# A delta-rule recurrence rewritten in 32-token chunks on small TensorE tiles, ahead of a mixture of experts

## The chip, the cores and the metric

The kernel runs on one NeuronCore of a Trainium2 chip. The engines are PE (TensorE, with its weight loads shown as PEld), DVE (VectorE), ACT (ScalarE), POOL (GpSimd) and SP, which here only issues DMAs and reads a few registers. The metric is device time in microseconds (us) of one execution; the kernel before took a median of 550.71 us in three runs (546.65 to 550.84).

## The reference

Attention by the delta rule, then a top-1 mixture of experts on its output. Everything is fp32. Batch 4, 8 heads, 768 tokens, head width 48; the model width is 8 x 48 = 384, with 8 experts of width 1024 and 3072 tokens in all.

```python
k_n = k / (norm(k) + 1e-6)
for t in range(S):                       # state: (B, H, 48, 48)
    y[:, :, t] = q_t @ state
    v_old      = k_n_t @ state
    state     += beta_t * outer(k_n_t, v_t - v_old)
x = y as 3072 rows of 384                # batch, token; heads side by side
logits = x @ w_gate + modality_bias[modality_id]
e = argmax(logits); g = softmax(logits)[e]
out = g * (relu(x @ w1[e]) @ w2[e])
```

Token by token the recurrence would be 768 serial steps. In chunks it becomes, per head: the Gram matrix of the chunk's keys, the inverse R of a unit triangular matrix made from it and beta, then Z = R (V - K S) with the state S before the chunk, Y = Q S + P Z with P the masked product of queries and keys, and S + K'Z for the next chunk.

## The kernel before

**Recurrence** (class `Attention`). A chunk is 64 tokens, so there are 12 chunks, each in two *group steps* of two batches and all heads: 24 steps `i=2c+g`. `gram` (L100 to L145) multiplies block-diagonal copies of the keys with keys and queries (L124, one matmul for two heads on the full array) and sorts the products into Gram blocks and P. `inverse_` (L154 to L238) works on sets of two chunks: six sets. Set 0 is inverted in blocks of 16 columns that `join` (L240) joins on PE with 32x32 and 16x32 tiles; the other five are inverted in blocks of 32 columns, one column after the other (L213 multiplies, L214 subtracts), rows 0 to 11 of the result on DVE and the rest on POOL. Sets 0 and 1 are laid out by transposes and copies, sets 2 to 5 go through DRAM (`GD`, `RD`, `RE`). `level_` (L314) joins blocks of 32 to blocks of 64 on PE (L326, L335). `chain_` (L348) is the serial part of a step: `ks` (K S, L363), `RHS` (V less it, DVE L365), `z` (L378), its copy `ZT` (ACT), the state's sum in PSUM (`Sps`, L386), its copy `Sbd` (ACT, L391), and beside it `y` (L372, L394), its copy `xo` and its store to DRAM (`xd`, L397). The two groups of a chunk have states of their own, so their chains can overlap. `route` sends each finished tile of 128 tokens through three transposes (L463) to the gate's logits (L468). Keys are loaded twice: once for the Gram products (`ke`) and once for the chain (`kqr`).

**Routing** (class `Router`). `rank` takes argmax, gate and the rank of each token in its expert. Tokens get places in lists for slots that hold one expert each: four of 512 tokens from the first 18 tiles (`part_a`, L579), then one of 512, two of 256 and one of 128 from the rest (`part_b`, L597). `lists` (L549) makes the lists by one-hot products on PE (L566).

**Experts** (class `Experts`). For each slot: gather rows (POOL indirect DMA, L657), transpose (L659), split tokens and weights in high and low parts, 9 matmuls per output block in layer 1 (L690; L710 for 128 tokens), 24 per 128 tokens in layer 2 (L733), scale (L736), scatter (L737). `tile_kernel` (L740) traces chain steps, levels, grams and inverses in one loop (L777 to L794), calls `part_a` after step 17 and `part_b` after step 23.

**What sets the order.** The program is traced in source order; a scheduler with a cost model then reorders instructions by priority and expected readiness and puts each engine's instructions in a fixed queue. `high_priority` lifts a block, `issue_after` puts the block's instructions behind a given one of the same engine. On the chip each engine takes its queue in order.

## Time and profile before

| | us |
|---|---|
| median of 3 runs | 550.71 |
| profiled execution, span | 550.4 |
| first / last z (L378) starts | 62.2 / 301.0 |
| first layer-1 matmul (L690) starts | 295.6 |
| PE / DVE / ACT / POOL busy | 483.5 / 364.5 / 263.5 / 208.5 |
| mean granted PE clock | 0.908 of full speed |

A row of the groups gives line, engine, operation, what is written from what, sizes, count, then busy time and the mean of one in ns, and last the engine's idle time just ahead of it with what ended it. In the timeline, a row starts with start and length in us, and `x16` means sixteen instructions merged into one row. Matmul records are pipelined: one record's length is mostly latency, and only the distance between starts is PE's time. An fp32 matmul shows as two records.

### The profile page before, as it was taken

The page shows a single profiled execution, that of the slowest core. Times are in us where ns is not written, and L with a number is a line of the kernel's source. Part 1 is how long each engine was busy: PE and PEld are TensorE (multiplying, and loading weights), DVE is VectorE, ACT ScalarE, POOL GpSimd, SP SyncE. Part 2 cuts the span into 40 slices and gives each one's busy share as a digit, 9 for nine tenths or more (in the row PEclk, how much of TensorE's full clock was granted, in tenths as well). Part 3 has the DMA queues.
Part 4 walks back from the last instruction along what each step waited for, and adds up shares of the span by engine and source line. Part 5 has one row for each costly group of instructions (what it writes and reads, how often), then busy time and mean ns, then how long its engine had stood idle before and what let it go on. Part 6 is the DMA issues. An engine that isn't in the chain of part 4 may idle for free. (4 is left out here: it accounts for less than half of the span.)

```text
span 550.4 us, 14025 instructions
## 1 busy us (share of the span) xinstructions
PE 483.5 (88%) x5459; PEld 432.1 (79%) x5459; DVE 364.5 (66%) x877; ACT 263.5 (48%) x619; POOL 208.5 (38%) x350
## 2 busy tenths in 40 slices
PE   7876875897898897998889997799999999999992
PEld 5776865786687776787768896689889898899992
DVE  5999899998789689577474499435536233437850
ACT  6855631655766567476565403043424334216540
POOL 9863477065066263111142136242303437111110
PEclk9977796588899799798889998699999999999997
DMA  8979741233594975838864224233623524427720
GB/s 205 247 200 238 176 105 55 64 95 89 169 226 138 236 180 166 209 120 230 228 192 142 76 80 127 75 116 114 209 79 120 170 75 164 128 78 227 233 85 9
DMA packets 82716, 80.81 MB, mean 147 GB/s; under 512 B 50105, under 2 KB 73671, under 8 KB 81520
## 3 DMA queue, kind: packets, MB, share of 16 engines
q1 hardware_dynamic: 79440, 70.18, 46.8%
q0 software_dynamic: 3200, 9.64, 5.2%
q8 instruction: 45, 0.74, 0.6%
q14 instruction: 31, 0.25, 0.2%
HBM read 65.12 MB, written 14.88 MB: 145 GB/s over the span
## 5 line engine op out<-in xcount | busy, mean ns | idle before, releaser
L733 PE MATMUL opa<-w2ha,h 128*128 128x384 f32 x256 | 69.1, 339 | 0.3 <-DVE ooa L736 0.3
L213 DVE TENSOR_TENSOR tm_x<-T,A 128x108 f32<-128x108 f32 (+12 forms) x165 | 57.8, 352 | 5.4 <-DVE PG L143 0.7
L124 PE MATMUL gp<-ke,KB 112*128 112x128 f32 x320 | 53.1, 331 | 9.3 <-DVE PG L143 3.9
L214 DVE TENSOR_TENSOR T<-T,tm_x 128x108 f32<-128x108 f32 (+12 forms) x165 | 56.8, 346 | 4.5
L124 PEld LDWEIGHTS gp<-ke,KB 112*128 112x128 f32 x320 | 48.3, 238 | 12.3 <-issue 3.7
L693 DVE SCALAR_TENSOR_TENSOR h<-hpa,h 128x512 fp32r<-128x512 f32 x32 | 22.0, 689 | 42.4 <-ACT h L692 42.4
L733 PEld LDWEIGHTS opa<-w2ha,h 128*128 128x128 f32 x256 | 46.2, 188 | 1.4 <-DVE ooa L736 0.5
L733 PE MATMUL opa<-w2la,h 128*128 128x384 f32 x128 | 43.0, 336 | 0.0
L692 ACT ACTIVATE h<-hpa 128x512 fp32r<-128x512 f32 x32 | 19.1, 596 | 49.5 <-PE hpa L690 49.5
L690 PE MATMUL hpa<-x,w1ha 128*128 128x512 f32 x144 | 39.1, 408 | 0.0
L340 POOL TENSOR_TENSOR kvn<-kvn,RR 128x384 f32<-128x384 f32 x22 | 18.7, 868 | 50.7 <-DMA kvn<-in_kv_dram 28.3
L363 PE MATMUL ks<-Sbd,kqr 112*64 112x96 f32 x352 | 27.3, 274 | 8.7 <-DMA kqr<-in_kq_dram 4.8
L365 DVE TENSOR_TENSOR RHS<-kvn,ks 64x384 f32<-64x384 f32 x44 | 24.2, 551 | 15.8 <-POOL kvn L340 9.4
L214 POOL TENSOR_TENSOR T<-T,tm_y 128x18 f32<-128x18 f32 (+8 forms) x90 | 30.7, 342 | 6.6
L213 POOL TENSOR_TENSOR tm_y<-T,A 128x18 f32<-128x18 f32 (+8 forms) x90 | 30.5, 339 | 6.6
L690 PEld LDWEIGHTS hpa<-x,w1ha 128*128 128x128 f32 x144 | 27.3, 194 | 5.5
L32 ACT COPY ZT<-z 64x384 f32<-64x384 f32 x48 | 22.7, 473 | 17.2 <-PE z L378 16.6
L363 PEld LDWEIGHTS ks<-Sbd,kqr 112*64 112x64 f32 x352 | 20.9, 150 | 11.8 <-ACT Sbd L32 4.4
L32 ACT COPY Sbd<-Sps 48x192 f32<-48x192 f32 x88 | 27.5, 313 | 5.2 <-PE Sps L386 2.7
L737 POOL DMA_INDIRECT out_dram<-ooa,sidxa x16 | 17.1, 1071 | 32.6 <-DMA out_dram<-ooa,sidxa 13.1
L657 POOL DMA_INDIRECT xga<-xd,gidxa x16 | 17.9, 1117 | 30.5 <-PE xpa L659 17.4
L378 PE MATMUL z<-RHS,R 128*64 128x96 f32 x384 | 26.9, 296 | 1.6 <-ACT R L338 1.6
(346 smaller groups left out, 1173.7 us busy)
## 6 DMA issues: line engine op xcount, KB each, us to landing
kvn<-in_kv_dram SPq DMA_DIRECT2D x12, 768.0 KB, 8.0
ke<-in_kq_dram SPq DMA_DIRECT2D x20, 448.0 KB, 6.8
kqr<-in_kq_dram SPq DMA_DIRECT2D x10, 896.0 KB, 6.9
w1ra<-in_moe_w_dram SPq DMA_DIRECT2D x16, 384.0 KB, 4.0
w2ra<-in_moe_w_dram SPq DMA_DIRECT2D x16, 384.0 KB, 3.2
xd<-xo SPq DMA_DIRECT2D x24, 192.0 KB, 2.5
w1rc<-in_moe_w_dram SPq DMA_DIRECT2D x8, 384.0 KB, 3.6
w2rc<-in_moe_w_dram SPq DMA_DIRECT2D x8, 384.0 KB, 3.2
```

The source lines that it names most:

```text
L32: if n=="scalar": nc.scalar.copy(o,i)
L124: nc.tensor.matmul(gp[p][:,j,:],KB[:,x,:],k[:,x].rearrange("r a t -> r (a t)"),start=True,stop=True)
L213: yield I.tensor_tensor(o,y,z,ALU.mult)
L214: yield I.tensor_tensor(x,x,o,ALU.subtract)
L340: if c: E(C.vq).tensor_tensor(V,V,w,ALU.mult)
L363: nc.tensor.matmul(ks[64*p:64*p+64,:,j,:],KQ[:,4*p+j,0],hc(Sb[:,4*p+j,:]),start=True,stop=True)
L365: b=64*p; nc.vector.tensor_tensor(RH[b:b+64,:,48*p:48*p+48].rearrange("q (h j) c -> q h j c",h=2),VN[b:b+64],ks[b:b+64],ALU.subtract)
L378: s.PI['z',i]=nc.tensor.matmul(z[64*h:64*h+64,:,j,:],R[:,2*j+h,:],hc(RH[:,4*h+j,:]),start=True,stop=True)
L690: nc.tensor.matmul(hp[:,v,:],w[:,k,fs],x[:,k,0:T],start=(n==0),stop=(n==8)); n+=1
L692: nc.scalar.activation(hh,hp,AF.Relu)
L693: nc.vector.scalar_tensor_tensor(hl,hp,0.0,hh.bitcast(F32),ALU.max,ALU.subtract)
L733: mm=nc.tensor.matmul(op,h[:,f%nf,ts_],w[:,f%2,:],start=(n==0),stop=(n==23)); n+=1
```

## The change

The recurrence is written anew. A chunk is 32 tokens, and all 32 pairs of batch and head are in one step: 24 chunk steps in a single chain. Rows of a tile are (batch, token), so every product is one of 32 small ones on its own part of the array: `ks`, `qs` and `gram` on tiles of 64 rows by 32 columns (batch picks the columns, head group the rows), `z` and `pz` on 32x32 tiles on the diagonal (batch picks both), `ds` (the state's change) on 32x64 tiles. The state is kept in SBUF, and DVE (`sv`, two batches) and ACT (`sa`; in PSUM it accumulates) write the next one.

All six sets (four chunks each) are inverted in blocks of 16 columns, 15 pairs of multiply and subtract (`sub`): set 0 on DVE, sets 1 to 5 on POOL. `jy`, `ya`, `jx`, `r1` join two blocks of 16 to one of 32 on PE, ACT, PE, DVE. The second level to 64 and the trip through DRAM are gone, and keys are loaded once.

The order is worked out in the source: `plan` lists tasks with engine, assumed duration, needs and priority, `Plan.order` plays them through, and `in_order` ties each engine's instructions of the recurrence to that order. Routing stays with the scheduler, but `part_a` now takes 20 of 24 tiles and is traced after the whole recurrence; logits are computed transposed, 32 experts wide, for four tiles at a time (`lg`). The first slot's PE instructions come behind PE's last one of the recurrence, its loads behind the last V load. Token rows in `xd` now have the reference's order, so `sidx` needs no arithmetic. The expert code is the same but for the buffers it uses. The host side lays `kq`, `kv`, `bblk`, constants, modalities and the padded gate weights out to match.

```diff
@@ head, planner @@
+NQ=11; SUBV=(0,); ZE=("ACT","ACT"); XE="ACT"; JD=.6; EPA=(0,1,2,3)
...
+    def order(s):
...
+            for e,w in waiting.items():
+                if busy.get(e,0)>now+1e-9 or not w: continue
+                w.sort(key=lambda t:(t["prio"],t["k"]))
+                for t in w:
+                    if all(free[r]>=v for r,v in t["take"].items()): break
+                else: continue
+                w.remove(t)
+                for r,v in t["take"].items(): free[r]-=v
...
+def in_order(tc,first):
+
+    last={}
+    for i in tc.nc.cur_bb.bb.instructions[first:]:
+        e=i.engine
+        if isinstance(i,mybir.Instruction) and type(i).__name__.startswith('BassTile'): continue
+        if e in last: tc.add_manual_dep(i,last[e].name,mybir.DependencyInfo(mybir.DependencyClass.NoSync,mybir.DependencyReason.DATA),reason="order")
+        last[e]=i
...
@@ Attention.plan @@
+        def gram(q,n):
+            if n==0: s.gp[q]=[s.mo(f"gp{q}_{h}") for h in range(2)]
             for j in range(4):
+                for b in range(4):
+                    for h in range(2):
+                        k=kr(2*q+n,h)
+                        mm(gv(s.gp[q][h])[32*b:32*b+32,n,j].rearrange("q a t -> q (a t)"),k[:,b,j,0],k[:,b,j].rearrange("r a t -> r (a t)"),start=True,stop=True)
...
+        for q in range(12):
+            m=q//2; pr=4*m-8+(q%2)*.5
+            for n in range(2): add(f"g{q}_{n}","PE",.48,lambda q=q,n=n: gram(q,n),[f"kq{2*q+n}",old("pz{}",2*q+1,10)]+([f"g{q}_0"] if n else [old("jy{}_11",m,2)]),prio=pr+.2*n,take=dict(mo=2) if n==0 else None)
+            add(f"ed{q}","ACT",.8,lambda q=q: ed(q),[f"g{q}_0",f"g{q}_1"]+([old("jy{}_11",m,2)] if q%2==0 else []),prio=pr+.3)
+            add(f"ep{q}","ACT" if q in EPA else "DVE",.85,lambda q=q: ep(q),[f"g{q}_0",f"g{q}_1","cst",old("pz{}",2*q+1,10)],prio=pr+.4)
+            if q in EPA: add(f"pm{q}","POOL",.95,lambda q=q: pm(q),[f"ep{q}","sub0_14"],prio=2*q-1.5)
+            add(f"gd{q}","-",0,lambda: None,[f"ed{q}",f"ep{q}"],lat=0,give=dict(mo=2))
+
...
+        def sub(m,c,E):
+            T=s.T[m]; na=c+1; n=15-c
+            o=s.pa.tile([128,2,64],F32,name=f"tm{m}_{c}",tag="tm",bufs=2)[:,:,0:na*n].rearrange("q k (a b) -> q k a b",a=na)
+            E.tensor_tensor(o,T[:,:,0:na,c:c+1].to_broadcast([128,2,na,n]),asub(s.A[m],c,c+1,16).to_broadcast([128,2,na,n]),ALU.mult)
+            x=T[:,:,0:na,c+1:16]; E.tensor_tensor(x,x,o,ALU.subtract)
+        def cs(m): V.tensor_tensor(s.T[m],s.T[m],s.t1[m].rearrange("q (k b) -> q k b",k=2).unsqueeze(2).to_broadcast([128,2,16,16]),ALU.mult)
...
+        def jy(m,p,k):
+            if k==0: s.jo[m,p]=s.mo(f"jo{m}_{p}")
+            for x in range(8*k,8*k+8):
+                for b in range(0,128,32): mm(s.jo[m,p][b:b+32,16*x:16*x+16],s.D[m][b:b+16,16*p+x],s.W1[m][b:b+16,16*p+x],start=True,stop=True)
+        def ya(m,p): A.activation(s.ya[:,16*p:16*p+16,0:16],s.jo[m,p][:,0:256].rearrange("q (x a) -> q x a",x=16),AF.Copy,scale=s.mn)
+        def jx(m,p,k):
+            for x in range(8*k,8*k+8):
+                for b in range(0,128,32): mm(s.jo[m,p][b:b+32,256+16*x:272+16*x],s.ya[b:b+32,16*p+x],s.W0[m][b:b+32,16*p+x],start=True,stop=True)
...
+        def r1(m,p): V.scalar_tensor_tensor(s.R[m][:,16*p:16*p+16,16:32],s.W0[m][:,16*p:16*p+16],s.m1,s.jo[m,p][:,256:512].rearrange("q (x a) -> q x a",x=16),ALU.mult,ALU.add)
...
+            e,E,f=("DVE",V,dv) if m in SUBV else ("POOL",G,po)
+            for c in range(15):
+                add(f"sub{m}_{c}",e,2*f(2*(c+1)*(15-c)),lambda m=m,c=c,E=E: sub(m,c,E),[f"n{m}",f"ti{m}"] if c==0 else [f"sub{m}_{c-1}"],prio=pr)
+            add(f"cs{m}","DVE",.7,lambda m=m: cs(m),[f"sub{m}_14"],prio=pr+.3)
...
+        def ks(c):
+            for j in range(4):
+                for b in range(4):
+                    for h in range(2): mm(hd(s.c2,h)[32*b:32*b+32,j],kr(c,h)[:,b,j,0],s.S[c][64*h:64*h+48,b,j],start=(j==0),stop=True,skip_group_check=True)
+        def qs(c):
+            for j in range(4):
+                for b in range(4):
+                    for h in range(2): mm(hd(s.y2,h)[32*b:32*b+32,j],kr(c,h)[:,b,j,1],s.S[c][64*h:64*h+48,b,j],start=(j==0),stop=False,skip_group_check=True)
+        def rh(c,h):
+            if h==0: s.tile("RH",c,[128,384],2)
+            z=slice(192*h,192*h+192); V.tensor_tensor(s.RH[c][:,z],s.KV[c][:,384:768][:,z],s.c2[:,h,0:192],ALU.subtract)
+        def z(c,h):
+            m,i=divmod(c,4); pp,n=divmod(i,2); rhs=s.RH[c] if c else s.KV[0][:,384:768]
+            for j in range(4):
+                for b in range(0,128,32): mm(hd(s.c2,h)[b:b+32,j],s.R[m][b:b+32,16*pp+8*h+4*n+j],rhs[b:b+32,192*h+48*j:192*h+48*j+48],start=(j==0),stop=True,skip_group_check=True)
+        def zt(c,h):
+            if h==0: s.tile("ZT",c,[128,384],3)
+            copy(nc,"scalar" if ZE[h]=="ACT" else "vector",s.ZT[c][:,192*h:192*h+192],s.c2[:,h,0:192])
+        def ds(c):
+            for j in range(4):
+                for b in range(4):
+                    o=(s.c2 if b<2 else s.s2)[:,b%2,0:192].rearrange("q (j e) -> q j e",j=4)
+                    for h in range(2):
+                        x=4*h+j; mm(o[64*h:64*h+64,j],s.KV[c][32*b:32*b+32,48*x:48*x+64],s.ZT[c][32*b:32*b+32,48*x:48*x+48],start=(b<2 and j==0),stop=True,skip_group_check=True)
+        def newS(c): return s.S[c] if c in s.S else s.tile("S",c,[128,4,4,48],2)
+        def sv(c):
+            o=newS(c+1)[0:112,0:2].rearrange("q b j e -> q b (j e)")
+            if c: V.tensor_tensor(o,s.S[c][0:112,0:2].rearrange("q b j e -> q b (j e)"),s.c2[0:112,:,0:192],ALU.add)
+            else: V.tensor_copy(o,s.c2[0:112,:,0:192])
...
+        def pz(c):
+            q,n=divmod(c,2)
             for h in range(2):
+                for j in range(4):
+                    for b in range(0,128,32): mm(hd(s.y2,h)[b:b+32,j],s.P[q][b:b+32,8*h+4*n+j],s.ZT[c][b:b+32,192*h+48*j:192*h+48*j+48],start=(c==0 and j==0),stop=True,skip_group_check=True)
+        def xo(c): copy(nc,"scalar" if XE=="ACT" else "vector",s.tile("xo",c,[128,2,192],3),s.y2[:,:,0:192])
+        def xd(c):
+            for b in range(4): nc.sync.dma_start(s.xd[768*b+32*c:768*b+32*c+32],s.xo[c][32*b:32*b+32].rearrange("q h e -> q (h e)"))
+        for c in range(NC):
+            m=c//4; top=-100+c
+            if c:
+                add(f"ks{c}","PE",.48,lambda c=c: ks(c),[f"sv{c-1}",f"sa{c-1}"],prio=top)
+                add(f"qs{c}","PE",.48,lambda c=c: qs(c),[f"sv{c-1}",f"sa{c-1}",old("xo{}",c,1)],prio=c-.5)
+            else: add("qs0","SP",0,lambda: None,["g0_0"])
             for h in range(2):
+                if c: add(f"rh{h}_{c}","DVE",.36,lambda c=c,h=h: rh(c,h),[f"ks{c}",f"vs{c}",old("z{}_1",c,2)],prio=top)
+                else: add(f"rh{h}_{c}","SP",0,lambda: None,["vs0"])
+                add(f"z{c}_{h}","PE",.36,lambda c=c,h=h: z(c,h),[f"rh{h}_{c}",f"r0_{m}",f"r1_{m}_{c//2%2}"]+([f"z{c}_0"] if h else []),prio=top)
+                add(f"zt{h}_{c}",ZE[h],.34,lambda c=c,h=h: zt(c,h),[f"z{c}_{h}",old("pz{}",c,3)]+([f"zt0_{c}"] if h else []),prio=top)
+            add(f"vs{c}","POOL",.9,lambda c=c: vs(c),[f"rrt{m}",f"kv{c}"]+(["sub0_14"] if m==0 else []),prio=c-2)
+            if c<NC-1:
+                add(f"ds{c}","PE",.45,lambda c=c: ds(c),[f"zt0_{c}",f"zt1_{c}"],prio=top)
+                add(f"sv{c}","DVE",.58,lambda c=c: sv(c),[f"ds{c}",old("qs{}",c,1)],prio=top)
+                add(f"sa{c}","ACT",.5,lambda c=c: sa(c),[f"ds{c}",old("qs{}",c,1)],prio=top)
+            add(f"pz{c}","PE",.7,lambda c=c: pz(c),[f"zt0_{c}",f"zt1_{c}",f"qs{c}",f"pm{c//2}" if c//2 in EPA else f"ep{c//2}"]+([f"xo{c-1}"] if c else []),prio=c-.3)
+            add(f"xo{c}",XE,.5,lambda c=c: xo(c),[f"pz{c}",old("xd{}",c,3),old("xt{}",c,3)],prio=c-.2)
+            add(f"xd{c}","SP",.24,lambda c=c: xd(c),[f"xo{c}"],prio=c-.2,mb=.2)
+            s.router.tasks(plan,s,c)
...
@@ Router.tasks, tile_kernel @@
+        def lg():
+            s.lg[u]=A.mo(f"lg{u}")[:,0:128]
+            for k in range(3):
+                for j in range(4): nc.tensor.matmul(s.lg[u][32*j:32*j+32],s.wg[:,k],A.xs[4*u+j][:,k],start=(k==0),stop=(k==2))
...
+    last=A.emit()
...
+    R.part_a(pa,sea,prt,pm,"mo")
+    R.rank(C.tA,24,prt,pm,"mo")
+    R.part_b(pb,seb,sec,see,prt,pm,"mo")
...
+            with after(PE_,A.load.ins): S=X.front(*x,env)
...
+        with after(PE_) if n==0 else contextlib.nullcontext(): X.layer1(S)
```

## The prediction

> **What bounds the kernel now.** I read the page's busy shares, then the windows view cut by stage, then the groups by line, then the chain of waits. The profiled execution took 550.4 us, the median of the runs shown is 550.71 us, so the sum below is made against 550.4 and needs no correction.

> ```profile
> PE 483.5 (88%) x5459; PEld 432.1 (79%) x5459; DVE 364.5 (66%) x877; ACT 263.5 (48%) x619; POOL 208.5 (38%) x350
> ```

> ```profile
> 0.00:62.00 62.00, 47.70 (x460) 42.90 (x460) 52.73 (x107) 40.98 (x135) 40.69 (x76) 0.86 0.91 223
> 62.00:302.00 240.00, 206.44 (x3723) 178.50 (x3724) 185.89 (x533) 137.94 (x353) 94.91 (x215) 0.86 0.58 155
> 302.00:352.00 50.00, 42.93 (x242) 39.05 (x241) 36.72 (x110) 12.82 (x22) 19.70 (x15) 0.91 0.32 99
> 352.00:541.00 189.00, 186.43 (x1037) 171.69 (x1036) 89.20 (x130) 71.74 (x111) 52.21 (x44) 0.99 0.42 131
> ```

> (Columns: length; busy time of PE, weight loads, DVE, ACT, POOL; clock; DMA share; GB/s.) Two kernels stand one behind the other. Until 302 us no engine is the bound alone: PE's 206 of 240 us are long records that overlap with waits, DVE has 186, and the clock is 0.86. From 352 us PE is full (186 of 189) and nothing but expert matmuls counts. The change rewrites the first kernel and leaves the second.

> ```profile
> L213 DVE TENSOR_TENSOR tm_x<-T,A 128x108 f32<-128x108 f32 (+12 forms) x165 | 57.8, 352 | 5.4 <-DVE PG L143 0.7
> L378 PE MATMUL z<-RHS,R x384: 246/246/423, 62.2 to 301.0; 128*64 128x96 f32 x192
> ```

> The recurrence's 24 steps run from the first z at 62.2 us to the last at 301.0: 10.4 us a step. The column eliminations of the inverses hold DVE for 57.8 us in L213 and nearly the same in L214, and a step is a row of short bursts that wait for each other across PE, ACT and DVE. The change removes all of L213, L214 on 32 columns, the second level of products per step (L326, L335), the block-diagonal key copies and the DRAM bounce of four of the six sets; it adds the 16-column eliminations, joins for every set, and three times the matmuls of a step on smaller tiles.

> ```profile
> 472.29 2.06 PE hpb L690 x9
> 474.35 1.06 PE opb L733 x6
> 485.81 0.35 PE hpc L690 x3
> 487.22 0.33 PE xpc L659 x3
> 535.78 4.27 PE ope L733 x23
> L566 PE MATMUL tpb<-l1b,l0b 128*128 128x88 f32 x48 | 9.3, 381 | 5.2 <-DVE l1b L564 5.2
> ```

> The chain of waits gives the price of the part that stays: 0.229 us for 512 columns, 0.177 for 384, 0.117 for 256, 0.11 for a transpose. A 512-token slot is 72 x 0.229 + 96 x 0.177 + 12 x 0.11 = 34.8 us, a 256-token slot 17.6, the 128-token slot 9.7; five, two and one of them are 219 us, before and after. Behind the last matmul (540.05) lie 10.3 us.

> **The change, part by part.** *Price of small tiles on PE.* An fp32 matmul is two records (192 z matmuls, x384).

> ```profile
> 73.66 0.73 PE L247 MATMUL jo<-W,D 16*32 16x16 f32 x64
> 77.36 0.73 PE L253 MATMUL jo<-ya,W 32*32 32x16 f32 x64
> 164.16 0.55 PE L463 MATMUL rxt<-ident,xo 128*128 128x128 f32 x3
> 164.63 0.88 PE L378 MATMUL z<-RHS,R 128*64 128x96 f32 x16
> 165.44 0.91 PE L468 MATMUL Sps<-wg,rxs 128*128 128x96 f32 x6
> 165.61 0.97 ACT L32 COPY ZT<-z 64x384 f32<-64x384 f32 x2 [0.34 <-PE z L378]
> 168.31 0.69 PE L335 MATMUL y<-R,ys 32*32 32x32 f32 x32
> L335 PE MATMUL y<-R,ys x768: 191/191/258, 60.6 to 294.7; 32*32 32x32 f32 x192
> L253 PE MATMUL jo<-ya,W x256: 177/209/231, 54.0 to 91.4; 32*32 32x16 f32 x128
> ```

> A burst less its last record, over the others, is the pitch. L335, two tiles at once, 32 columns: (0.69 - 0.19)/31 = 16 ns, so 32 ns per record on its own tile. z, two tiles, 96 columns: (0.88 - 0.246)/15 = 42, so 84 per tile. Between them: 45 ns for 48 columns, 58 for 64. L253, four tiles, 16 columns: (0.73 - 0.19)/63 = 8.6 ns. The new products of 48 columns run on eight tiles (ks, qs, ds: 64x32 and 32x64) or four (z, pz: 32x32). No row shows eight. From one side 45/8 = 5.6 ns, from the other 8.6 (the jo row); I take 7. With four: 45/4 = 11. [...]

> *PE per chunk (24 of them, 32 tokens of all 32 heads).* ks, qs, ds: 3 x 64 records x 7 = 1.35 us. z, pz: 2 x 64 x 11 = 1.41. Gram: 64 records of 64 columns, 58/8 = 7: 0.45. Joins of the 16-blocks: 512 records per four chunks, 128 x 8.6 = 1.10. Transposes 0.35 (the 0.55 of three, less the tail). Logits: 24 records per four chunks on 128x32 tiles, 0.17. Sum 4.8 us, 521 records. Whenever the tile shape changes PE pauses: the last z record starts at 164.63 + 0.88 - 0.246 = 165.26, the next line at 165.44, 0.18 us against a pitch of 0.04. Of 4 (the chain's own) to 12 changes a chunk I take 8 at 0.12: 5.8 us. At a clock between the window's 0.86 and 1 it is 5.8 to 6.7; I take 6.25.

> *The chain per chunk*, ks, rh, z, zt, ds, sv, next ks:

> ```profile
> L33 DVE COPY D<-gp 128x128 f32<-128x128 f32 x8 | 2.1, 289 | 5.3 <-ACT PG L126 5.3
> L143 DVE TENSOR_TENSOR PG<-gp,um 128x256 f32<-128x256 f32 x16 | 6.6, 416 | 1.5 <-ACT gd L32 1.2
> L126 ACT COPY PG<-gp 128x128 f32<-128x128 f32 x48 | 12.5, 270 | 21.7 <-PE gp L124 21.5
> L142 ACT COPY PG<-gp 128x256 f32<-128x256 f32 x32 | 12.1, 386 | 0.5 <-DVE D L33 0.4
> L365 DVE TENSOR_TENSOR RHS<-kvn,ks 64x384 f32<-64x384 f32 x44 | 24.2, 551 | 15.8 <-POOL kvn L340 9.4 <-PE ks L363 5.6 <-issue 0.2
> L32 ACT COPY xo<-y 128x384 f32<-128x384 f32 x24 | 11.5, 478 | 0.5
> L165 DVE STREAM_TRANSPOSE A<-D 128x1024 f32<-128x1024 f32 x2 | 3.9, 1952 | 0.0
> L176 DVE RECIPROCAL t<-s 128x32 f32<-128x32 f32 x6 | 2.1, 348 | 2.6 <-ACT s L175 2.5
> L213 POOL TENSOR_TENSOR tm_y<-T,A 128x18 f32<-128x18 f32 (+8 forms) x90 | 30.5, 339 | 6.6
> L340 POOL TENSOR_TENSOR kvn<-kvn,RR 128x384 f32<-128x384 f32 x22 | 18.7, 868 | 50.7 <-DMA kvn<-in_kv_dram 28.3 <-DVE tm_x L213 11.2 <-ACT rxs L465 9.0
> ```

> rh of 192 columns lies between 0.29 and 0.42: 0.35, twice. zt between 0.27 and 0.39: 0.33. sv 0.55 (L365). ks 0.45, the second z 0.35, ds 0.45, each with a last record of 0.2. Five hops of 0.1 (z ends at 164.63 + 0.88 = 165.51, its ACT copy starts at 165.61). Together 0.65 + 0.70 + 0.55 + 0.33 + 0.65 + 0.55 + 0.5 = 3.9 us, some 5 when each step waits for a filler in front of it. PE's 6.25 is longer, so PE's load sets the pace, and with imperfect filling I take 6.7 us for 20 chunks; the last four have no grams and joins, 4.5. The other engines lie beside it. DVE per four chunks: transposes 1.95 + 1.0 + 1.0, seven small steps at most 0.35 and two row scalings 0.42, column scaling 0.7, r1 0.8, rh and sv 5.0, masks of P 1.7: 15.5 of 26.8. POOL: 30 eliminations x 0.34, four V scalings x 0.87, a fill 0.9: 14.6. ACT: zt 0.66, sa, xo, xs 0.48 each, D copies 0.39, 0.35 of join copies: 2.85 a chunk. SP: four xd writes instead of one, 24 x 0.85 MB of loads in place of the keys twice and the bounce of the inverses through DRAM; 0.85 MB in 6.7 us is 127 GB/s, below the 223 of the first window. The expert weights follow the last V load on SP; the first of them waits there for the expert's number from part a, and only xd writes, with three buffers, can stand behind it. In the routing, the logits come transposed (a 128x128 copy and a 32-block transpose per four chunks, 0.6 us), one load of the modalities replaces four and five small index steps go: nothing on the path but 0.5 us.

> *Prologue.*

> ```profile
> 168.56 0.26 DVE L213 TENSOR_TENSOR tm_x<-T,A 128x96 f32<-128x96 f32 x1
> kqr<-in_kq_dram SPq DMA_DIRECT2D x4, 448.0 KB, 4.7
> ```

> Four key loads (1.84 MB at 223 GB/s, 8.2 us, behind 4 of issue and latency: 4.7 less the load's own 2.0, and the small loads ahead) 12.3; gram 0.75; D copies 0.8; transpose 1.95; square root 0.35; norms 3.2; 30 eliminations of 91 columns on average, 0.25 each, 7.5; scaling 0.7; W1 1.0; join 1.4 + 0.4 + 1.4 + 0.4; twelve hops 1.2. The first z at 34 us, against 62.2. The warm-up matmuls that go are hidden by the loads (0.5 us at most if not).

> *End of recurrence.* 34 + 20 x 6.7 + 4 x 4.5 = 186, less 6 for grams and joins that PE did in the prologue, plus 3 for the last pz, copy and logits: 183 us.

> *Hand-over.* Before, part a starts with 18 of 24 tiles and hides under the chain:

> ```profile
> 247.16 0.23 DVE L477 TENSOR_TENSOR L<-Sps,btok 128x72 f32<-128x72 f32 x1 [2.54 <-PE Sps L468]
> 281.92 0.17 DVE L577 TENSOR_TENSOR sidxa<-tfa,tf2a 128x16 int32<-128x16 f32 x1
> 295.64 1.67 PE L690 MATMUL hpa<-x,w1ha 128*128 128x512 f32 x6
> ```

> 35 us on a shared DVE; with DVE half free I take 22 (from 17, its own steps, to 35). Now it needs 20 tiles of 24, whose logits exist about 14 us before the end: it ends 8 us behind it. The gathers, transposes and splits took 14 us among chain work; 10 free. Layer 1 is put behind the last recurrence instruction on PE anyway. PE idles some 18 us, and experts start at 201.

> *Sum.* 201 + 219 + 9.3 (list matmuls, L566) + 4 (list waits; PE's idle from 302 to 352 was 7) + 10.3 = 444 us.

> **Rivals.** *Faster filling:* clock 1 and four shape changes: 5.3 a chunk, 20 x 1.4 = 28 and about 4 of hand-over less: 412. For: more PE work per us than before, and the clock is 0.99 where PE is full. Against: the chain's own gaps.

> *Row tiles that share columns don't overlap:* ks, qs, gram then run four-way (0.70, 0.70, 0.93), ds two-way (1.44). 2.0 us more a chunk: 444 + 20 x 2.0 x 1.08 + 4 x 1.5 = 493. Neither for nor against: all bursts before have one row tile per column tile.

> *PE's instructions don't arrive in time (the slower side).*

> ```profile
> q8 instruction: 45, 0.74, 0.6%
> xd<-xo SPq DMA_DIRECT2D x24, 192.0 KB, 2.5
> ```

> 45 packets fed PE's 10,918 instructions, 243 each; each took 0.006 x 16 x 550/45 = 1.2 us of an engine. A chunk now has 1042, 4.3 packets: at 1.2 us they hide (5.2 of 6.7). If each is asked for only when the last is used up, it costs a landing; for xd that is 2.5 us. At t a packet the total is 444 + 20 x (4.3 t - 6.7) + 4 x (2.7 t - 4.5): it reaches 550 at t = 2.7, and 3.2 gives 602. Against: 64 jo records, 128 instructions, passed without a hole.

> [...]

> *The order fixed in the source is wrong:* the plan gives the norms 1.4 us where the rows give 3.2, and a queue that waits for a set's inverse holds the chain behind it. Five sets by up to 10 us: 494.

> **How the numbers follow.** Forecast 444 us: 0.55. Faster filling 0.12, no overlap in columns 0.16, wrong order 0.08, late instructions 0.05, bank turns and the 25 ns floor 0.04. The range takes in 412, 493 and 494 with a little on top: 405 to 500. Under 1% cannot be told from no change in a measurement of this kernel. Only late instructions, bank turns and the floor end at or above 550: slower 0.07, within 1% 0.02, faster 0.91. It does what it says in any case: the old eliminations of 32 columns are gone.

> **What would show it.** z first at about 34 us; the last state update near 180; ks bursts of 64 records of about 0.65 us (0.9 without overlap); PE over 85% busy between, clock over 0.9; a hole of some 18 us in PE before the first hpa near 201; then 243 us as before. Wrong if PE idles inside chunks with DVE or POOL late, if holes follow the instruction packets, or if the experts no longer fill PE.

## The result and the profile after

The change makes the kernel slower: 681.16 us (median; 676.42 to 684.41) against 549.62 us (546.65 to 550.84), a ratio of 1.238, 95% interval 1.229 to 1.246. The forecast was 444 us, with a range of 405 to 500. The profiled execution took 676.42 us, with a span of 674.7.

First the page of the changed kernel: busy time of each engine, its granted clock in 40 slices, the instruction queue, the chain, and some groups (busy and mean ns, then the idle time before them with its releaser).

```profile
PE 489.8 (73%) x13631; PEld 434.9 (64%) x13631; DVE 232.8 (35%) x535; ACT 164.3 (24%) x327; POOL 168.7 (25%) x286
...
PEclk9999999955565565757556655699899999999997
...
q8 instruction: 109, 1.79, 1.1%
...
PE 68%; issue 18%; DVE 7%; DMA 3%; ACT 1%; SPq 0%; POOL 0%; POOLq 0%; DVEq 0%; ACTq 0%
...
L129 PE MATMUL gp<-kq 48*32 48x64 f32 x1536 | 30.8, 307 | 29.3 <-issue 19.3
...
L230 PE MATMUL c<-RH,R 32*32 32x48 f32 x1472 | 36.2, 266 | 12.6 <-issue 12.4
...
L226 DVE TENSOR_TENSOR RH<-KV,c 128x192 f32<-128x192 f32 x46 | 14.2, 350 | 79.9 <-PE c L219 55.8
L185 PE MATMUL jo<-W,ya 32*32 32x16 f32 x1536 | 26.7, 210 | 19.7 <-issue 19.7
```

Before, PE had 5459 records; now it has 13,631. The instruction queue went from 45 packets to 109, of 16.4 KB each (1.79 MB / 109). PE is the engine that everyone waits for (RH on VectorE waits 55.8 us for ks), yet PE's own idle time is mostly put down to "issue": the profile shows nothing that PE waited for there. The chain has 18% of it.

The next rows are windows of the same kernel (length; busy time and records of PE, weight loads, VectorE, ScalarE, GpSimd; clock; DMA share; GB/s), by the stages of the prediction, then two slices of 25 us.

```profile
36.40:52.40 16.00, 7.58 (x507) 7.19 (x511) 5.47 (x12) 1.91 (x4) 5.55 (x14) 1.00 0.03 6
52.40:386.40 334.00, 225.46 (x11282) 194.65 (x11274) 72.10 (x169) 62.61 (x159) 71.26 (x169) 0.67 0.21 58
386.40:437.50 51.10, 23.77 (x128) 21.27 (x128) 38.02 (x165) 8.36 (x14) 8.51 (x9) 0.53 0.36 108
...
75.00:100.00 25.00, 17.44 (x893) 15.36 (x894) 9.95 (x22) 5.95 (x15) 7.40 (x21) 1.00 0.27 75
...
275.00:300.00 25.00, 13.55 (x896) 12.31 (x896) 5.22 (x17) 4.09 (x10) 11.65 (x31) 0.61 0.11 29
...
437.50:674.70 237.20, 222.56 (x1219) 203.56 (x1219) 98.67 (x145) 84.74 (x131) 71.55 (x59) 0.97 0.40 126
```

The recurrence has 334 us from the first z to the last pz, where the prediction had 149. VectorE, ScalarE and GpSimd together are busy for 206 us of it. The two slices show what holds it: 893 and 896 records in 25 us, once at clock 1.00 and once at 0.61, with different work in each. Over the 334 us it is 11,282 records, 29.6 ns each. A pace that depends neither on the clock nor on what is computed speaks against TensorE's array as the bound; the experiments below test it.

The timeline of PE in one chunk shows how the time passes (start, length, record, count; in brackets the idle time before it):

```profile
72.87 0.60 PE L219 MATMUL c<-S,kq 48*32 48x48 f32 x21
75.37 0.73 PE L219 MATMUL c<-S,kq 48*32 48x48 f32 x38 [1.90 <-issue]
...
76.76 0.56 PE L223 MATMUL y<-S,kq 48*32 48x48 f32 x19
79.38 0.81 PE L223 MATMUL y<-S,kq 48*32 48x48 f32 x42 [2.06 <-issue]
80.11 1.50 PE L230 MATMUL c<-RH,R 32*32 32x48 f32 x64
...
86.61 0.96 PE L219 MATMUL c<-S,kq 48*32 48x48 f32 x60
```

ks breaks off in the middle, 1.90 us pass, and it goes on; so does qs, 4.0 us later. The profile shows nothing that the second part waited for, and the same line had run just before. Between the two resumptions lie the rest of ks, a gram and a third of qs, 128 records by the counts of the timeline. Each record is a weight load and a matmul, two instructions (the page counts 13,631 of each), so that is 256 instructions, and 27,262 instructions in 109 packets are 250 a packet. That fits a PE that runs out of instructions once a packet.

The sum, in the prediction's stages: first z at 52.4 instead of 34 (+18), recurrence 334 instead of 149 (+185), 51 us between last pz and first hpa instead of 18 (+33), the rest 239 instead of 243 (-4). 444 + 232 = 676.

### The profile page after: what moved, and what is told of

Same layout as the page of the kernel before. It is cut to its first block, busy times and chain, and to the rows that moved or that the text cites. A ratio compares the mean times of both kernels' runs of the same rounds, so it can differ in the third digit from the quotient of the medians.

```text
span 674.7 us, 29526 instructions
## 1 busy us (share of the span) xinstructions
PE 489.8 (73%) x13631; PEld 434.9 (64%) x13631; DVE 232.8 (35%) x535; ACT 164.3 (24%) x327; POOL 168.7 (25%) x286
## 3 DMA queue, kind: packets, MB, share of 16 engines
q8 instruction: 109, 1.79, 1.1%
## 4 chain that ended last, share of the span: by engine, by line
PE 68%; issue 18%; DVE 7%; DMA 3%; ACT 1%; SPq 0%; POOL 0%; POOLq 0%; DVEq 0%; ACTq 0%
PE hpa L570 10%; PE opa L613 10%; PE c L230 5%; PE y L250 5%; PE jo L185 4%; PE jo L181 3%; PE c L219 3%; PE gp L129 3%; PE y L223 3%; PE c L239 3%; PE rxt L342 3%; PE hpc L570 3%; PE hpb L570 3%; PE opc L613 2%; PE opb L613 2%
## 5 line engine op out<-in xcount | busy, mean ns | idle before, releaser
L129 PE MATMUL gp<-kq 48*32 48x64 f32 x1536 | 30.8, 307 | 29.3 <-issue 19.3
L250 PE MATMUL y<-ZT,P 32*32 32x48 f32 x1536 | 37.8, 266 | 12.6 <-issue 12.1
L230 PE MATMUL c<-RH,R 32*32 32x48 f32 x1472 | 36.2, 266 | 12.6 <-issue 12.4
L243 DVE TENSOR_TENSOR S<-S,c 112x384 f32<-112x384 f32 x22 | 12.1, 551 | 94.4 <-PE s L239 32.9
L181 PE MATMUL jo<-W,D 16*32 16x16 f32 x1536 | 25.3, 207 | 25.4 <-issue 20.1
L250 PEld LDWEIGHTS y<-ZT,P 32*32 32x32 f32 x1536 | 31.6, 151 | 16.6 <-issue 14.0
L230 PEld LDWEIGHTS c<-RH,R 32*32 32x32 f32 x1472 | 30.8, 154 | 17.5 <-issue 16.0
L226 DVE TENSOR_TENSOR RH<-KV,c 128x192 f32<-128x192 f32 x46 | 14.2, 350 | 79.9 <-PE c L219 55.8
L185 PE MATMUL jo<-W,ya 32*32 32x16 f32 x1536 | 26.7, 210 | 19.7 <-issue 19.7
L181 PEld LDWEIGHTS jo<-W,D 16*32 16x32 f32 x1536 | 23.1, 146 | 27.4 <-issue 26.8
L169 POOL TENSOR_TENSOR tm<-T,A 128x30 f32<-128x30 f32 (+7 forms) x75 | 26.7, 356 | 51.4 <-DVE A L160 45.9
L219 PE MATMUL c<-S,kq 48*32 48x48 f32 x1472 | 26.3, 270 | 16.9 <-issue 14.5
L185 PEld LDWEIGHTS jo<-W,ya 32*32 32x32 f32 x1536 | 24.2, 151 | 22.0 <-issue 21.4
L573 DVE SCALAR_TENSOR_TENSOR h<-hpa,h 128x512 fp32r<-128x512 f32 x32 | 22.1, 690 | 44.5 <-ACT h L572 44.5
L239 PE MATMUL c<-ZT,KV 32*64 32x48 f32 x736 | 28.3, 292 | 10.1 <-issue 8.1
## 6 DMA issues: line engine op xcount, KB each, us to landing
kq<-in_kq_dram SPq DMA_DIRECT2D x24, 448.0 KB, 4.5
```

The source lines that it names most:

```text
L129: mm(gv(s.gp[q][h])[32*b:32*b+32,n,j].rearrange("q a t -> q (a t)"),k[:,b,j,0],k[:,b,j].rearrange("r a t -> r (a t)"),start=True,stop=True)
L169: E.tensor_tensor(o,T[:,:,0:na,c:c+1].to_broadcast([128,2,na,n]),asub(s.A[m],c,c+1,16).to_broadcast([128,2,na,n]),ALU.mult)
L181: for b in range(0,128,32): mm(s.jo[m,p][b:b+32,16*x:16*x+16],s.D[m][b:b+16,16*p+x],s.W1[m][b:b+16,16*p+x],start=True,stop=True)
L185: for b in range(0,128,32): mm(s.jo[m,p][b:b+32,256+16*x:272+16*x],s.ya[b:b+32,16*p+x],s.W0[m][b:b+32,16*p+x],start=True,stop=True)
L219: for h in range(2): mm(hd(s.c2,h)[32*b:32*b+32,j],kr(c,h)[:,b,j,0],s.S[c][64*h:64*h+48,b,j],start=(j==0),stop=True,skip_group_check=True)
L230: for b in range(0,128,32): mm(hd(s.c2,h)[b:b+32,j],s.R[m][b:b+32,16*pp+8*h+4*n+j],rhs[b:b+32,192*h+48*j:192*h+48*j+48],start=(j==0),stop= ...
```

## The experiments

The theory that this profile suggests is F: TensorE's instructions come at one packet of 256 per 3.65 us (128 records at the 28.5 ns that one took), and nothing else matters in the recurrence. The rivals are T, the array's work on small tiles, and D, the chain through the other engines. Four kernels tell them apart.

**A third of the columns, the same instructions.** In ks, qs, z, pz and ds:

```diff
-mm(hd(s.c2,h)[32*b:32*b+32,j],kr(c,h)[:,b,j,0],s.S[c][64*h:64*h+48,b,j],start=(j==0), ...
+mm(hd(s.c2,h)[32*b:32*b+32,j,0:16],kr(c,h)[:,b,j,0],s.S[c][64*h:64*h+48,b,j,0:16],start=(j==0), ...
```

> The changed kernel with the five products of the recurrence (ks, qs, z, pz, ds) fed 16 moving columns instead of 48; the other 32 columns of each head are left out, everything else and every instruction count stay. Theory F (TensorE's instructions arrive too slowly: one packet of 256 instructions every 3.65 us): the recurrence doesn't move, its last pz stays at 386 us within 6 us. Rival T (TensorE's own work on small tiles: tiles that don't overlap, or half the clock): 7488 of the 12096 records lose two thirds of their columns; at the 28.5 ns that a record takes now that is up to 140 us, so an end before 320 us. Rival D (the chain through the other engines in the fixed order): no more than 10 us, the others' instructions are the same.

**Twice the instructions, the same columns.**

```diff
-for h in range(2): mm(... ,j], kr(c,h)[:,b,j,0], s.S[c][64*h:64*h+48,b,j], ...)
+for h in range(2):
+    for w in (0,24): mm(... ,j,w:w+24], kr(c,h)[:,b,j,0], s.S[c][64*h:64*h+48,b,j,w:w+24], start=(j==0 and w==0), ...)
```

> The changed kernel with each of the five products of the recurrence issued as two matmuls of 24 moving columns instead of one of 48: the same result, the same columns in all, 7488 records (14976 TensorE instructions) more. Theory F: 58.5 packets more at 3.65 us: the last pz goes from 386 to about 600 us, the time from 676 to about 890. Rival T: the same columns, at most 7 ns for each added record: 386 to at most 440. Rival D: 386 to at most 400, as the other engines do the same.

**One pass instead of two.**

```diff
-mm=nc.tensor.matmul
+up=lambda a: a.bitcast(BF)[:,1::2] if len(a.shape)==2 else ...   # upper half of each float
+def mm(o,w,x,**k): return nc.tensor.matmul(o,up(w),up(x),**k)
```

> The changed kernel with the recurrence's small matmuls reading the upper 16 bits of each float as bf16, so that each is one pass instead of two: half of the TensorE instructions, lower precision, everything else the same. Theory F: 48 packets instead of 96, 175 us instead of 350 behind the first ones: the last pz at 210 to 230 us, total about 500 to 520; the packets still come every 3.65 us. Rival T: array time halves too, so the same direction, but the packets then come at no fixed spacing. Rival D: the end stays within 30 us of 386.

**Without the joins of five sets.**

```diff
 def jy(m,p,k):
     if k==0: s.jo[m,p]=s.mo(f"jo{m}_{p}")
+    if m:
+        if k==0: mm(s.jo[m,p][:,0:256],s.zz[:,0:128],s.zz,start=True,stop=True)
+        return
```

> The changed kernel without the joins of the inverses (jy, jx) in the sets 1 to 5: one matmul with a zero operand stands for each 64 of them, so the two halves of a chunk are not coupled; all else is the same. It has 5040 TensorE instructions fewer, 19.7 packets. Theory F: 19.7 x 3.65 = 72 us less, last pz at about 314 us. Rival T: 2520 records at 8.6 ns (clock 1) to 17 ns (half clock) = 22 to 43 us less. Rival D: less than 15 us, the joins are off the state's chain.

What was measured. The first fence is the changed kernel, the others are the four runs in this order: the row of the pz matmuls (count, ns, first and last start; the line number moves with the edit), then the instruction queue, and for the narrow run the clock.

```profile
L250 PE MATMUL y<-ZT,P x1536: 198/276/285, 57.9 to 386.1; 32*32 32x48 f32 x192
```

```profile
PEclk9999999999999999999999999999899999989998
...
q8 instruction: 109, 1.79, 1.1%
...
L250 PE MATMUL y<-ZT,P x1536: 178/209/232, 57.2 to 382.8; 32*32 32x16 f32 x192
```

```profile
q8 instruction: 167, 2.74, 1.3%
...
L255 PE MATMUL y<-ZT,P x3072: 191/223/245, 62.8 to 600.8; 32*32 32x24 f32 x192
```

```profile
q8 instruction: 61, 1.00, 0.9%
...
L108 PE MATMUL y<-ZT,P x768: 178/210/219, 39.8 to 211.2; 32*32 32x48 bf16 x192
```

```profile
q8 instruction: 89, 1.46, 1.0%
...
L256 PE MATMUL y<-ZT,P x1536: 198/276/285, 59.5 to 318.8; 32*32 32x48 f32 x192
```

| run | PE instructions | last pz, us | expected by F | time, us | ns per instruction changed |
|---|---|---|---|---|---|
| changed kernel | | 386.1 | | 676.4 | |
| a third of the columns | 0 | 382.8 | 386 | 676.5 | |
| two matmuls for one | +14,976 | 600.8 | 600 | 889.8 | 214.7 / 14,976 = 14.3 |
| one pass | -12,096 | 211.2 | 210 to 230 | 505.4 | 174.9 / 12,096 = 14.5 |
| no joins in five sets | -5,040 | 318.8 | 314 | 611.7 | 67.3 / 5,040 = 13.4 |

Each of the four ran once; four runs of the changed kernel spread over 8 us, far less than the differences read here. Two thirds of the columns left out moved the last pz by 3.3 us; instructions cost 13.4 to 14.5 ns each, whichever they were: 3.4 to 3.7 us for 256. T falls with the first run and D with the other three, since the other engines' instructions were the same in all of them. A fixed 14 ns that TensorE itself spends on every instruction would fit these four runs as well; it doesn't fit the bursts (the 60 ks records above, 120 instructions, start within 0.96 - 0.28 = 0.68 us), and the stream below decides it. The narrow run also settles the clock. Its granted clock is 0.9 or more all through the recurrence, the changed kernel's is in the slices from 135 to 439 us between 0.5 and 0.8, and the two take the same time. The half clock is not the cause.

The single-pass version is also faster than the kernel before, at the lower precision of its products. It was timed again:

> The single-pass version (bf16 halves) once more, timed against the kernel before: one look gave 505 us beside 554. Theory F: 0.91 to 0.92 of the kernel before; the other theories say nothing new here.

It took 503.86 us (502.65 to 506.05) against 551.62 (550.62 to 556.33), a ratio of 0.911, interval 0.905 to 0.917. It gets its instructions no faster, a packet per 3.9 us in the trace of its first run; it needs half as many in the recurrence.

**The supply by itself.** A stream of small independent matmuls between long ones, without and with loads beside it:

```diff
+long(200); short(sm,1536)                 # nothing else moves
+long(200); loads of all keys and values; short(s2,1536)
+long(200); wide(fp,1024)                  # two passes, 48 columns
```

> Nothing of the model is computed: TensorE runs 200 long matmuls (128 rows, 512 bf16 columns), then 1536 small ones of one pass (eight tiles of 48x32, 8 columns each, 3072 instructions, 12 packets) with no data moving; 200 long ones; the same 1536 small ones while the key and value loads run; 200 long ones; 1024 records of two-pass matmuls of 48 columns on the eight tiles. Theory F, in its plain form (the next packet of 256 instructions is asked for when the one before it starts, and takes a fixed time to come): both small stretches take 12 x 3.65 = 44 us, and after each long stretch, where packets have time to come, the first hole comes after one or two packets (128 to 256 records). Form F2 (the packets share the DMA engines with the data): the quiet stretch is well under 44 us and the loaded one over it. Rival T (array time): at 7 ns a record the small stretches take 11 us, and the last one 7.

Rows of its timeline on PE: the quiet stretch, the loaded one, and the stretch of two-pass matmuls. Then two of its windows (columns as above): quiet, and loaded.

```profile
47.18 1.36 PE L26 MATMUL sm<-a 48*32 48x8 bf16 x151
51.26 1.18 PE L26 MATMUL sm<-a 48*32 48x8 bf16 x128 [2.73 <-issue]
...
55.27 1.18 PE L26 MATMUL sm<-a 48*32 48x8 bf16 x128 [2.82 <-issue]
...
90.74 0.99 PE L26 MATMUL sm<-a 48*32 48x8 bf16 x105 [2.82 <-issue]
...
136.40 1.83 PE L26 MATMUL s<-a 48*32 48x8 bf16 x207
140.38 1.18 PE L26 MATMUL s<-a 48*32 48x8 bf16 x128 [2.15 <-issue]
148.22 1.18 PE L26 MATMUL s<-a 48*32 48x8 bf16 x128 [6.66 <-issue]
153.87 1.18 PE L26 MATMUL s<-a 48*32 48x8 bf16 x128 [4.47 <-issue]
...
240.88 2.57 PE L32 MATMUL fp<-a 48*32 48x48 f32 x263
245.62 1.36 PE L32 MATMUL fp<-a 48*32 48x48 f32 x128 [2.18 <-issue]
```

```profile
46.00:92.00 46.00, 15.19 (x1541) 13.68 (x1542) 0.17 (x1) 0.00 (x0) 0.55 0.02 4
...
136.00:182.00 46.00, 10.49 (x1106) 9.43 (x1104) 0.92 (x2) 0.00 (x0) 0.53 0.96 229
```

Here nothing else can be waited for, and the holes come after exactly 128 records, 256 instructions. Quiet, a packet comes every (90.74 - 51.26) / 10 = 3.95 us on the mean, of which it runs for 1.2, and the 3072 instructions took 44.5 us. F's plain form had 44, which is partly luck: the distance was longer than its 3.65, and the first 151 records found their instructions ready. In the stretch of two-pass matmuls, quiet as well, the shortest distance was 3.45. Beside loads of 229 GB/s it is 5.4 to 7.8 us, and the stretch took 58.5 instead of 44: F2 is right in that the distance was longer beside the loads, and wrong in that the quiet stretch didn't come well under 44. After the stretches of long matmuls 151, 207 and 263 records passed before the first hole, so up to two packets were ahead of PE. At 1.2 us for 256 instructions, 4.6 ns each, a fixed 14 ns of TensorE's own is excluded.

The packets' transfers are in the traces too. In the quiet stretch there is one at a time: it begins 1.1 to 1.7 us after a burst has begun, takes 0.9 to 1.4, and the next burst begins 1.3 to 1.5 us after it has landed (landed at 53.86, burst at 55.27). Beside the loads the transfer is no longer (on the mean of the run's 36 packets it takes 0.009 x 16 x 281.8 / 36 = 1.1 us); it begins later, 2.6 to 5.2 us after the burst. So the transfer is only a third of the quiet distance. In the changed kernel's recurrence 89 packets come 3.8 us apart on the mean, with transfers of 0.9 to 1.5, and of PE's 70 holes over 0.6 us between matmuls, 66 end 1.1 to 1.8 us after a packet has landed; in the recurrence of the kernel before it is 4 of 20. What sets a packet off isn't in the records. That it is asked for when the one before it starts to run, as in F's plain form, was the author's assumption; what is seen is that a transfer can begin before the burst ends: in the joins of the changed kernel's first set a burst of 1.90 us begins at 48.24, the transfer runs from 49.39 to 50.68, and the next burst begins at 51.97. The changed kernel's recurrence, with a DMA share of 0.21, lies near the quiet end.

In the changed kernel's expert units nothing of this shows: 1219 records in 237 us are 25 us for 256 instructions, and no matmul's wait there is put down to issue. In the quiet stretch 1.2 of every 4 us was execution, and for the rest PE waited for the next packet.

**The hand-over.** In the changed kernel and in all four runs of the first set, 50 to 51 us lie between the last pz and the first hpa. Rows of the changed kernel's timeline, VectorE first, then PE:

```profile
368.84 0.32 DVE L368 TENSOR_TENSOR OH<-nz,mx 128x160 f32<-128x160 f32 x1
```

```profile
387.84 2.12 PE L347 MATMUL lg<-xs,wg 128*32 128x128 f32 x24
389.90 0.90 PE L371 MATMUL pt<-OH,ones 128*128 128x160 f32 x2
...
427.01 1.98 PE L452 MATMUL tpb<-l1b,l0b 128*128 128x88 f32 x8 [12.23 <-DVE l1b L450]
428.79 0.85 PE L541 MATMUL xpa<-ident,xga 128*128 128x128 f32 x3
```

Part a's one-hot rows are ready at 369.2, but its first product stands behind the recurrence's last instruction on PE and starts at 389.9. Later the transposes of the gathered tokens stand behind part b's first list product, for which PE waits 12.2 us. Two edits on the single-pass version test this. The first moves the last ranks and part b behind the first unit's layer 1; the second also emits part a's steps among the last chunks.

```diff
-    R.rank(C.tA,24,prt,pm,"mo")
-    R.part_b(pb,seb,sec,see,prt,pm,"mo")
 ...
         with after(PE_) if n==0 else contextlib.nullcontext(): X.layer1(S)
+        if n==0:
+            R.rank(C.tA,24,prt,pm,"mo")
+            R.part_b(pb,seb,sec,see,prt,pm,"mo")
```

> The single-pass version (bf16 halves) with the rest of the routing (the ranks of the last four tiles and part b, its stages, look-ups and list products) put behind the first expert unit's layer 1 in the source. In the single-pass run, the changed kernel and the split and join runs alike, 50 us lie between the last pz record and the first layer-1 matmul. Theory H: part b's VectorE chain, which fills 417 to 427 us there and stands in TensorE's queue before the transposes of the gathered tokens, costs some 10 of these: 38 to 41 us remain, total 505 to about 495. Rival: the gathers and weight splits end last anyway, 47 to 50 us remain, total within 4 us of 505.

```diff
         for t in p.order():
             t["fn"]()
+            if t["name"]=="lt4": bg=hook          # part a as a generator
+            if bg and t["eng"]=="DVE":
+                for _ in range(8): next(bg,None)
```

> As the run with part b moved, and the steps of part a (ranks, places and lists of the first 20 tiles) are emitted in the last chunks, eight steps with each VectorE task of the plan from the one on that transposes the logits of the 20th tile; its two products write free columns of a PSUM tile of the recurrence. Theory H: part a's first product no longer stands behind the recurrence's last instruction on TensorE (21 us from its operand's being ready to its start in the changed kernel). The last pz comes 5 to 10 us later, since VectorE takes part a's steps in between, and the first layer-1 matmul 15 to 22 us behind it instead of 50: total 475 to 490. Rival: VectorE in its fixed order holds the recurrence for as long as the hand-over gains: total within 5 us of the run with part b moved.

In the single-pass run the last pz is at 211.2 and the first hpa at 261.4. With part b moved they are at 210.0 and 248.6: the 12 us are won as H said, but the total is 512.0, not 495. This row of that run shows where they went: TensorE now waits 14.5 us for the same product behind the first unit's layer 1.

```profile
282.44 1.98 PE L454 MATMUL tpb<-l1b,l0b 128*128 128x88 f32 x8 [14.46 <-DVE l1b L452]
```

With part a in the last chunks too, the last pz is at 232.4 and the first hpa at 254.9, only 22.5 behind it; but the recurrence has become 22 us longer. In its last part VectorE runs part a's steps between the chain's, and TensorE waits 8.2 us for part a's operands and 9.6 us for ScalarE's copies of the chain. The total is 518.3, 6.3 above the run before: H (475 to 490) missed, and the rival, which gave at most 5, was nearer. A third place for part b, behind the first unit's layer 2 and the second's transposes, was timed:

> The single-pass version with the ranks of the last four tiles and part b put behind the first expert unit's layer 2 and the second unit's transposes in the source, so that their list products stand among the matmuls of the second unit. Put behind layer 1 they held TensorE for 14.5 us, which used up the 12 us that the hand-over had won. Theory H: here VectorE's chain has the time of a whole unit, about 33 us, before the first of them is due: the 38.6 us between last pz and first layer 1 stay, no hole over 3 us inside the units, total 12 us under the single-pass run, about 493. Rival: the chain of part b, sharing VectorE with the h and token copies of the second unit, delays that unit as much: within 4 us of it.

It took 501.21 us (498.64 to 504.16), 0.905 of the kernel before (0.899 to 0.911), 2.65 us from the single-pass version, whose range it overlaps: H's 493 missed, and the rival's "within 4 us" held. The first hpa came at 248.9 there, 14.4 earlier than in the single-pass run beside it (263.3), and the stretch from it to the end is 253.5 us long instead of 241.0. PE is busy for 8.3 us more of it (232.1 instead of 223.8), with part b's products now among the units, and a layer-1 matmul waits 4.3 us for VectorE. Three ways of reordering moved the work of the hand-over elsewhere and won at most 3 us; whether another order would win more was not tried.

## Why the prediction was wrong

*The step that failed* is the pace of a chunk: "PE's 6.25 is longer, so PE's load sets the pace", 6.7 us for 20 chunks. It came from the time that records take on the array, and the supply of instructions was set aside as a rival with a chance of 0.05, for two reasons. The first, "at 1.2 us they hide", took the time that a packet's bytes keep a DMA engine busy for the time between packets; what was measured is 3.4 to 4.0 us between packets, three times as long, of which the transfer is a third. The second, "64 jo records, 128 instructions, passed without a hole", was too short a burst to say anything: in the stream up to two packets, 512 instructions, lay ready (263 records, 526 instructions, passed before a hole). The kernel before fed 45 packets in 550 us; in its trace no two of them begin less than 3.4 us apart. That doesn't show that they couldn't, but nothing there supported 1.2. The rival's own formula, at 3.7 us a packet, gives 444 + 20 x (15.9 - 6.7) + 4 x (10.0 - 4.5) = 650. Late instructions were named, as a rival, and the price formula comes near the measured 676; the price taken was the one that hid it.

*The array's prices* were too low as well, though that cost nothing that shows in the time here. In a burst of the stream 263 two-pass records of 48 columns on eight tiles took 2.57 us, (2.57 - 0.28) / 262 = 8.7 ns each, and 60 of ks in the changed kernel 0.96, (0.96 - 0.28) / 59 = 11.5 ns, where 7 was taken; 64 z records in 1.50 us are (1.50 - 0.27) / 63 = 19.5 ns where 11 was taken. That a third of the columns takes the same total time in the narrow run shows that they weren't the bound.

*The first z*, 52.4 instead of 34: the joins took 16 us of it (507 records, four packets' worth) where 3.6 were predicted, for the same reason. The remaining 6 us lie ahead of the joins: 3.3 of them are a hole in the grams of the first set, put down to issue again, the rest lies in the chain of the first inverse behind them.

*The hand-over*, 51 instead of 18: the step "it ends 8 us behind it" assumed that part a could run while the last chunks did. Its first product is behind them on PE's queue, 21 us after its operand; and "10 free" left out part b's chain ahead of the token transposes, for which PE waits 12.9 us.

*The experts*, 239 us with what follows, against 243: near, but partly by luck. The 243 held 13 us for list products and their waits, and 40 of the 48 products ran in the hand-over instead; the units took 226 us from the first layer-1 matmul to the last matmul where 219 were predicted.

*The other rivals.* Row tiles that share columns: 0.70 us for 64 ks records, 11 ns, was the price without overlap. The stream's 8.7 is below it, the changed kernel's 11.5 is not, so this stays open; it isn't what the kernel waits for. No run shows the two terms that share a chance of 0.04, bank turns and the 25 ns floor: the z records start 19.5 ns apart, those of ks 11.5, and the stream's one-pass records (1.18 - 0.18) / 127 = 7.9. A wrong order in the source was not what held the recurrence: with half of the instructions the same order runs in 171 us (39.8 to 211.2).

*What the list of signs said.* The sign "if holes follow the instruction packets" is what happened. "PE over 85% busy between, clock over 0.9" failed too (67% and 0.67), but names no cause: PE is busy for 67% of the recurrence only because a record that waits for nothing still counts its 0.27 us.

## What to carry to other kernels

Count TensorE's instructions as well as its columns: a matmul of two passes was four of them here (1536 records for the 768 pz matmuls, each with its weight load), and in these runs PE waited for its program where its instructions would have taken less than some 14 ns each (3.4 to 3.7 us for 256), with 16, 24 and 48 columns alike. Take the price of a packet from the distance between packets (3.8 us in the changed kernel), not from its transfer (0.9 to 1.5). The sign in these profiles was idle time put down to issue that cut a single line in two, after 128 records each time where nothing else could be waited for, and at the same pace whatever the work and the clock (893 and 896 records in 25 us, at 1.00 and 0.61). The cure is fewer instructions for the same work: one pass was shown here (505.4 us instead of 676.4), wider tiles or more columns each were not tried. An experiment that changes columns and instructions separately tells the two limits apart in two runs.

## What was not expected of the hardware

The granted clock fell to about 0.5 in stretches where PE waited for its instructions (0.55 and 0.53 in the two windows above), but stayed at 0.9 or more in the narrow run's recurrence at the same pace of instructions. What sets it stays open; it made no difference to the time here.
